# Layer two's weight conversions ordered behind the rectified tiles on ScalarE

## The chip, the cores and the metric

The kernel runs on one core of a Trainium2 chip. The metric is the device time of one launch in microseconds (us), the median of the runs that are shown. Five engines work beside each other: TensorE (PE, with its weight loads as PEld), VectorE (DVE), ScalarE (ACT), GpSimd (POOL) and SyncE (SP), which starts most transfers. Each engine executes its own instructions strictly in the order in which they were put.

## The reference

Three steps, all in float32:

```python
# 1. retention attention, 2 batches x 8 heads x 768 tokens x 64, in 12 blocks of 64 tokens
intra = (qb @ kb.T * Dmask) @ vb
inter = (qb * lam_pow) @ kv_state
out[block] = intra + inter
kv_state = lam_block * kv_state + (kb * rev_pow).T @ vb
# 2. x: (2, 768, 512), mixed by two Fourier transforms, then layer one
u = x + real(fft(fft(x, axis=1), axis=2))
un = (u - mean(u)) / sqrt(var(u) + 1e-6)
x = u + maximum(un @ w_ch1, 0) @ w_ch2          # 512 -> 2048 -> 512
# 3. layer two, with a gain g_ln and weights of its own
xn = (x - mean(x)) / sqrt(var(x) + 1e-6) * g_ln
return x + maximum(xn @ w_ch1, 0) @ w_ch2
```

## The kernel before

**Tiling.** The 1536 tokens are four blocks of 384. Each of the two layers runs over its four blocks, and each block over the 16 groups `f` of 128 hidden units. One step of that is a `unit(n)`, n = 0 to 127: layer n // 64, block n // 16 % 4, group n % 16. The last block of layer one is n = 48 to 63; names of it carry `0_3`, those of the first block of layer two `1_0`. A float32 operand is held as two float16 tiles, a high and a low part, and a product is three matmul passes over them.

**The way up.** `mlp_up_fast` (L826) takes two groups at once with seven block products in place of eight. I call two such groups a pair, and number the eight pairs of a block from 0 (pair k is f = 2k and 2k + 1). A product is 6 matmuls of 192 columns (L845) into two PSUM tiles: "left" holds the first 192 tokens (`ps_1...`, as `ps_11_0_12` for layer 1, block 0, f = 12), "right" the others (`ps_2...`). In the second half of a pair, ahead of `rest`, come product three and the product "12" into left, then VectorE forms `t` from left (L865) and adds it into right (L866). `rest` then puts the last left product (`th,w`) and the last right product (`unT,sw`), VectorE adds to left (L871) and to right (L872), ScalarE rectifies left and right into the high part of `h` (L877), and VectorE computes the low part (L878). So L865 reads what the last left product overwrites, and L866 what the last right product adds to.

**The way down.** `mlp_down` puts, three units later, the matmuls of 512 columns that read `h` (L892), 9 for a group.

**Sums.** The seven products need sums of weights (`w1_sums`: L790 on VectorE, L791 to L793 and L797 on GpSimd, L796 on ScalarE) and of normalized tokens (`un_sums`: L805, L810 to L813 on VectorE, L820 on ScalarE, L821 on GpSimd). A block's tokens are normalized before it starts: L706 and L714 on ScalarE, L715 on GpSimd, then transposes by SP into `unT`.

**Conversions.** Weights come from memory 512 columns at a time and are turned into high and low float16 parts by `conv_steps`, whose steps go from engine to engine: ScalarE L301 and L302 (into a PSUM tile), VectorE L304, ScalarE L326 (the gain, for layer two's first matrix) and L327 (high part), GpSimd L329 (low part). Layer two has 16 conversions of its first matrix (`w1_unit`, every second one followed by `w1_sums`) and 16 of its second. Six of the latter (`AWAY`) are made early in the kernel, stored to memory and loaded back; ten are converted in the stretch that this case is about.

**The order.** A list scheduler places every instruction on its engine in the order of a modelled time, by priority and by dependences. Background work is put at a unit number by `put` and recorded in the middle of that unit, after the pair's first products and before `mlp_down` and `rest`. `gate["relu"]` is the last rectification (L877) recorded so far; `tc.issue_after(x)` bars everything recorded under it from being placed ahead of x on ScalarE. Before, the conversions ran under `later`, which leaves them their priority and asks for no order; only the stagings of the six early tiles (`staged_late`) stood behind the rectification.

Of the kernel before, what the change touches and what calls it, by code (L numbers as in the profile page):

```python
# [51 lines left out]
EARLY0, GATEN, B1, SPC, DS, DC, DFO, DD, D1S, D2S, AO, YA, NR, NE, LN1, L1, L2, F01, F02, TL, R1, R2, SE, PR1, LAG, UB, FB, NW, MQ, SPL = 11, 8, 6, 2.0, 2.0, 5, 1.0, 0.5, 0.5, 1.0, "aba", "aa", 2, 0, 3, 2.5, 2.5, 16, 4, 3, 1.5, 2, "dddd_dppp", 0, 3, 3, 13, 11, 1, 3  # L52
# [3 lines left out]
AWAY = {0: 37, 2: 39, 4: 41, 6: 43, 8: 45, 10: 47}  # L56
# [67 lines left out]
def tile_retention_fourier_mlp(ctx: ExitStack, tc: tile.TileContext, a: dict, out: bass.AP):  # L124
# [28 lines left out]
    def hl(name):  # L153
        return fp.tile([P, 2, 512], F16, tag="f", name=name)
# [116 lines left out]
    def run(steps):  # L271
        for t in steps:
            pass
        return t

    def w_conv(kind, m, i):
        return run(conv_steps(kind, m, i, "at"))

    def w_stage(i):
        t = hl(f"wst2_{i}")  # L280
        run(conv_steps(2, 1, i, "at", t))
        away[i] = dram.tile([P, 2, 512], F16, name=f"wd{i}")
        sp.dma_start(away[i], t)

    def w_back(i):
        w2t[1, i] = wpool.tile([P, 2, 512], F16, tag=f"w2_{i}", name=f"w2_1_{i}")
        sp.dma_start(w2t[1, i], away[i])
# [393 lines left out]
    unT, unt, gate = {}, {}, {}  # L681
# [90 lines left out]
    def w1_sums(m, g, kk, r=None):  # L772
        w = w1t[m, g]
        i = (2 * g + kk - 2) % 8
        if 3 <= i < 7:
            t = const.tile([P, 2, 2, 2, 256], F16, tag=f"big{i - 3}", name=f"sw{m}_{g}_{kk}")
            t = [t[:, 0], t[:, 1]]
        elif i < 3:
            t = [ldp.tile([P, 2, 2, 256], F16, tag="ld", name=f"sw{m}_{g}_{kk}_{x}") for x in range(2)]
        else:  # L780
            t = [const.tile([P, 2, 2, 256], F16, tag=f"state{x}", name=f"sw{m}_{g}_{kk}_{x}") for x in range(2)]
        if r is None:
            r = [f32t(f"wr{m}_{g}_{k}") for k in (kk, kk + 2)]
            for x, k in enumerate((kk, kk + 2)):
                dve.tensor_tensor(r[x], w[:, 0, k], w[:, 1, k], op=ALU.add)  # L785
        eng = [pool if z == "p" else dve for z in SE.split("_")[m]]
        (a11, a21), (a12, a22) = ([z.rearrange("p (q a f) -> p q a f", a=2, f=P)[:, :, x] for x in range(2)] for z in r)
        s12, s34 = (f32t(f"ws{x}_{m}_{g}_{kk}") for x in (12, 34))
        s1, s2, s3, s4 = (z[:, x * 256:x * 256 + 256].rearrange("p (q f) -> p q f", f=P) for z in (s12, s34) for x in range(2))
        eng[0].tensor_tensor(s1, a21, a22, op=ALU.add)  # L790
        eng[1].tensor_tensor(s2, s1, a11, op=ALU.subtract)  # L791
        eng[2].tensor_tensor(s3, a11, a21, op=ALU.subtract)
        eng[3].tensor_tensor(s4, a12, s2, op=ALU.subtract)  # L793
        for x, z in enumerate((s12, s34)):
            hi, lo = (t[x][:, y].rearrange("p s f -> p (s f)") for y in range(2))
            act.copy(hi, z)  # L796
            pool.tensor_tensor(lo, z, hi, op=ALU.subtract)  # L797
        sw[m, g, kk] = t
# [254 lines left out]
    def put(n, task):  # L1053
        bg.setdefault(max(int(n), 0), []).append((n, len(bg), task))

    def later(task, offset):
        def run():
            with tc.high_priority(offset=-offset):
                task()
        return run  # L1060
# [21 lines left out]
    n = t + DC + DFO  # L1082
# [25 lines left out]
    n0 = (NB - 1) * NF  # L1108
    first = {}

    def w1_unit(p):
        g, kk, half = p // 4, p % 4 // 2, p % 2
        t = w_conv(1, 1, 4 * g + kk + 2 * half)
        if not half:
            first[g, kk] = t
        else:
            w1_sums(1, g, kk, (first.pop((g, kk)), t))

    for i in range(NF):
        put(n0 + 4 + R1 * i, later(lambda i=i: w1_unit(i), PR1))  # L1120
        put(n0 + 3.5 + R2 * i, later(lambda i=i: w_back(i) if i in AWAY else w_conv(2, 1, i), PR1))
    def staged_late(i):
        with tc.issue_after(gate["relu"].ins):
            w_stage(i)

    for i, n in AWAY.items():
        put(n, lambda i=i: staged_late(i))

    def step(n):
        m = n // (NB * NF)  # L1130
# [59 lines left out]
```

## Time and profile before

| | us |
|---|---|
| median of 3 runs | 589.38 |
| lowest and highest run | 588.20, 590.11 |
| profiled execution | 589.12 |
| its span | 587.3 |
| granted TensorE clock, mean share of full | 0.996 |
| PE busy | 568.8 (97%) |
| DVE busy | 390.1 (66%) |
| ACT busy | 279.9 (48%) |
| POOL busy | 280.7 (48%) |

All times of the profile run from the start of the span. The launch takes 1.8 us more than the span. The conversions of layer two lie between 293 and 400 us, in which layer one's last block ends (at some 340 us) and layer two's first block runs (to about 398 us). Busy shares over the whole span say that PE is the engine that is nearly always at work; what the others delay can be seen only as gaps on PE.

### The profile page before, as it was taken

The page shows a single profiled execution, that of the slowest core. Times are in us where ns is not written, and L with a number is a line of the kernel's source. Part 1 is how long each engine was busy: PE and PEld are TensorE (multiplying, and loading weights), DVE is VectorE, ACT ScalarE, POOL GpSimd, SP SyncE. Part 2 cuts the span into 40 slices and gives each one's busy share as a digit, 9 for nine tenths or more (in the row PEclk, how much of TensorE's full clock was granted, in tenths as well). Part 3 has the DMA queues.
Part 4 walks back from the last instruction along what each step waited for, and adds up shares of the span by engine and source line. Part 5 has one row for each costly group of instructions (what it writes and reads, how often), then busy time and mean ns, then how long its engine had stood idle before and what let it go on. Part 6 is the DMA issues. An engine that isn't in the chain of part 4 may idle for free.

```text
span 587.3 us, 11862 instructions
## 1 busy us (share of the span) xinstructions
PE 568.8 (97%) x4655; PEld 378.3 (64%) x4655; DVE 390.1 (66%) x868; ACT 279.9 (48%) x561; POOL 280.7 (48%) x294
## 2 busy tenths in 40 slices
PE   7889999999999999999999999999999999999997
PEld 5745645566554555676676676776767677767775
DVE  6998898766976449678767768666536453544333
ACT  3667779733332334455497787953223132312110
POOL 8935799985452564454476876952112100210000
PEclk8999999999999999999999999999999999999999
DMA  8998079960000010253265442700110025002001
GB/s 285 368 397 335 2 252 262 340 203 3 1 1 0 19 37 18 73 127 108 83 206 179 133 156 84 168 19 2 64 28 19 1 88 57 20 1 88 22 2 54
DMA packets 47014, 63.23 MB, mean 108 GB/s; under 512 B 26224, under 2 KB 29166, under 8 KB 46958
## 3 DMA queue, kind: packets, MB, share of 16 engines
q1 hardware_dynamic: 46142, 62.27, 34.2%
q8 instruction: 36, 0.59, 0.4%
q10 hardware_dynamic: 816, 0.21, 0.2%
q14 instruction: 20, 0.16, 0.1%
HBM read 52.23 MB, written 6.29 MB: 100 GB/s over the span
## 4 chain that ended last, share of the span: by engine, by line
PE 65%; DVE 12%; ACT 6%; POOL 6%; DMA 5%; issue 5%; SPq 1%; DVEq 0%; POOLq 0%; ACTq 0%
PE ps_y L892 30%; PE ps L845 22%; PE ps_h L752 6%; DMA k<-in_k 3%; POOL w L329 2%; PE ps_d L551 1%; ACT w L327 1%; POOL sw L797 1%; DVE wr L785 1%; PE ps_y_at L892 1%; PE ps_y_dn L892 1%; DMA cdsd<-in_cd 1%; DMA ws<-in_w 1%; ACT top L310 1%; DVE u L918 1%
## 5 line engine op out<-in xcount | busy, mean ns | idle before, releaser
L892 PE MATMUL ps_y<-w,h 128*128 128x512 f16 x1104 | 271.6, 379 | 2.4 <-ACT h L877 1.6
L892 PEld LDWEIGHTS <-h 128*128 128x128 f16 x1200 | 113.8, 98 | 100.6 <-ACT h L877 3.7
L845 PEld LDWEIGHTS <-sw 128*128 128x128 f16 x1104 | 94.5, 98 | 15.8 <-issue 3.0
L845 PE MATMUL ps<-th,sw 128*128 128x192 f16 x828 | 91.1, 246 | 1.1 <-DVE wf L304 0.7
L845 PEld LDWEIGHTS <-w 128*128 128x128 f16 x828 | 72.0, 98 | 17.1 <-issue 0.2
L877 ACT ACTIVATE h<-ps 128x384 f16<-128x384 f32 x92 | 43.6, 488 | 80.6 <-DVE ps L871 76.1
L329 POOL TENSOR_TENSOR w<-wf,w 128x512 f16<-128x512 f32 x58 | 66.8, 1160 | 22.6 <-ACT w L327 22.3
L752 PE MATMUL ps_h<-unT,w 128*128 128x384 f16 x396 | 72.5, 326 | 1.0 <-ACT w L327 0.8
L845 PE MATMUL ps<-unT,w 128*128 128x192 f16 x552 | 62.9, 246 | 0.0
L878 DVE SCALAR_TENSOR_TENSOR h<-ps,h 128x384 f16<-128x384 f32 x92 | 49.2, 554 | 13.9 <-ACT h L877 12.2
L752 PEld LDWEIGHTS <-w 128*128 128x128 f16 x396 | 37.6, 98 | 29.9 <-ACT w L327 1.7
L865 DVE TENSOR_TENSOR t<-ps,s 128x192 f32<-128x192 f32 x46 | 16.3, 354 | 54.0 <-PE ps L845 54.0
L797 POOL TENSOR_TENSOR sw<-ws,sw 128x512 f16<-128x512 f32 x32 | 37.0, 1173 | 21.2 <-ACT sw L796 21.2
L715 POOL TENSOR_TENSOR uns<-un,uns 128x512 f16<-128x512 f32 x21 | 25.2, 1198 | 39.3 <-ACT uns L714 39.3
L694 POOL TENSOR_TENSOR rs<-rs,neghalf 128x1 f32<-128x1 f32 x24 | 14.4, 603 | 61.9 <-DVE rs L692 59.6
L327 ACT CAST w<-wf 128x512 f16<-128x512 f32 x58 | 35.2, 611 | 11.9 <-DVE wf L314 8.8
L821 POOL TENSOR_TENSOR th<-ts,th 128x384 f16<-128x384 f32 x24 | 22.1, 939 | 38.8 <-ACT th L820 38.8
L857 ACT COPY s<-ps 128x192 f32<-128x192 f32 x46 | 14.4, 313 | 53.8 <-PE ps L845 53.7
L871 DVE TENSOR_TENSOR ps<-ps,s 128x192 f32<-128x192 f32 x46 | 16.6, 360 | 29.3 <-PE ps L845 29.1
L379 POOL TENSOR_TENSOR m<-m,m 128x512 f16<-128x512 f32 x24 | 31.5, 1327 | 4.7 <-ACT m L377 4.6
L304 DVE SCALAR_TENSOR_TENSOR wf<-ws,ps_w 128x512 int32<-128x512 int32 x34 | 23.2, 684 | 14.8 <-ACT ps_w L302 8.8
L767 DVE SCALAR_TENSOR_TENSOR h<-ps_h,h 128x384 f16<-128x384 f32 x36 | 19.7, 550 | 18.7 <-ACT h L766 18.6
(176 smaller groups left out, 851.1 us busy)
## 6 DMA issues: line engine op xcount, KB each, us to landing
ws<-in_w SPq DMA_DIRECT2D x25, 511.8 KB, 5.4
ws<-in_w2b SPq DMA_DIRECT2D x16, 511.8 KB, 4.3
ws<-in_w1b SPq DMA_DIRECT2D x16, 511.8 KB, 3.9
kt<-in_kt SPq DMA_DIRECT2D x12, 256.0 KB
qt<-in_qt SPq DMA_DIRECT2D x12, 256.0 KB, 5.3
v<-in_v SPq DMA_DIRECT2D x12, 256.0 KB
k<-in_k SPq DMA_DIRECT2D x12, 256.0 KB, 5.2
pre<-in_w SPq DMA_DIRECT2D x4, 511.8 KB
```

Of the source, the lines that this page charges most:

```text
L304: dve.scalar_tensor_tensor(ti, raw[:, :, 0], 13, part.bitcast(I32), op0=ALU.logical_shift_right, op1=ALU.bitwise_or)
L327: act.copy(hi, t)
L329: gate["lo"] = pool.tensor_tensor(lo, t, hi, op=ALU.subtract)
L379: pool.tensor_tensor(t[:, 1], m32, t[:, 0], op=ALU.subtract)
L715: pool.tensor_tensor(s_[:, 1], un, s_[:, 0], op=ALU.subtract)
L752: pe.matmul(ps, w[:, i, k, fo:fo + P], x[:, j, k, :], start=n == 0, stop=n == 11)
L797: pool.tensor_tensor(lo, z, hi, op=ALU.subtract)
L821: pool.tensor_tensor(t[:, 1], z, t[:, 0], op=ALU.subtract)
L845: pe.matmul(ps, lhs, rhs, start=start and n == 0, stop=n == 5, skip_group_check=True)
L877: gate["relu"] = act.activation(hi, z, AF.Relu)
L878: dve.scalar_tensor_tensor(lo, z, 0.0, hi, op0=ALU.max, op1=ALU.subtract)
L892: pe.matmul(ps, h[:, x, j * P:(j + 1) * P], w[:, y, c], start=f == 0 and n == 0, stop=f == NF - 1 and n == 2)
```

## The change

All 16 conversions of the first matrix and the 10 of the second now run under `issue_after(gate["relu"].ins)`, as the stagings did. The loads of the six stored tiles (`w_back`) lose `later` too. No operation is added or taken away; what each engine executes is put in another order.

```diff
+    def behind_relu(task, i):
+        with tc.issue_after(gate["relu"].ins):
+            task(i)
+
     for i in range(NF):
-        put(n0 + 4 + R1 * i, later(lambda i=i: w1_unit(i), PR1))
-        put(n0 + 3.5 + R2 * i, later(lambda i=i: w_back(i) if i in AWAY else w_conv(2, 1, i), PR1))
-    def staged_late(i):
-        with tc.issue_after(gate["relu"].ins):
-            w_stage(i)
-
+        put(n0 + 4 + R1 * i, lambda i=i: behind_relu(w1_unit, i))
+        put(n0 + 3.5 + R2 * i, lambda i=i: w_back(i) if i in AWAY else behind_relu(lambda i: w_conv(2, 1, i), i))
     for i, n in AWAY.items():
-        put(n, lambda i=i: staged_late(i))
+        put(n, lambda i=i: behind_relu(w_stage, i))
```

Here `n0` is 48, `R1` is 1.5 and `R2` is 2, so that a conversion of the first matrix is put every 1.5 units from unit 52 on, and one of the second at every second unit from 51 on.

On ScalarE, in layer two's first block, these rows stand between the right rectification of pair 1 (h1_0_1 from ps_21_0_2) and the left one of pair 2 (h1_0_2 from ps_11_0_4). Names end in a buffer number; `half`, `ps_w` and `wf` are tiles of a conversion (`1_1_12` is the twelfth of layer two's first matrix, `2_1_9` one of its second), `sw` is a sum of weights, `un` and `uns` are normalized tokens. Before:

```order
L877 ACTIVATE h1_0_1_4901<-ps_21_0_2_4814 128x2x192
L706 ACTIVATE un1_1_0_4982<-u0_119,rs1_1_0_4933 128x512
L796 CAST sw1_2_1_4947<-ws34_1_2_1_4949 128x512
L302 CAST ps_w1_1_12_5057<-half1_1_12_5056 128x512
L714 CAST uns1_1_0_4986<-un1_1_0_4982 128x512
L857 COPY s1_0_6_5030<-ps_11_0_6_5031 128x192
L301 ACTIVATE half1_1_13_5206<-ws1_1_13_5203 128x512
L326 ACTIVATE wf1_1_12_5055<-wf1_1_12_5055,gcol_187 128x512
L302 CAST ps_w1_1_14_5102<-half1_1_14_5101 128x512
L877 ACTIVATE h1_0_2_5025<-ps_11_0_4_4907 128x2x192
```

After, behind the same right rectification of pair 1:

```order
L301 ACTIVATE half1_1_11_4939<-ws1_1_11_4936 128x512
L301 ACTIVATE half2_1_9_4994<-ws2_1_9_4991 128x512
L302 CAST ps_w1_1_11_4940<-half1_1_11_4939 128x512
L302 CAST ps_w2_1_9_4995<-half2_1_9_4994 128x512
L326 ACTIVATE wf1_1_11_4938<-wf1_1_11_4938,gcol_187 128x512
L327 CAST w2_1_9_4999<-wf2_1_9_4993 128x512
L327 CAST w1_1_2_4722<-wf1_1_11_4938 128x512
L706 ACTIVATE un1_1_0_4982<-u0_119,rs1_1_0_4933 128x512
L796 CAST sw1_2_1_4947<-ws12_1_2_1_4948 128x512
L714 CAST uns1_1_0_4986<-un1_1_0_4982 128x512
L857 COPY s1_0_6_5030<-ps_11_0_6_5031 128x192
L877 ACTIVATE h1_0_2_5025<-ps_11_0_4_4907 128x2x192
```

Eleven instructions stand between the two rectifications in place of eight, seven of them a whole stage of two conversions; and conversion 11 stands where 12 to 14 stood before.

On PE, pair 6 of the same block: the rows from the end of the product "12" (`unT,w` into `ps_11_0_12`) on. `ps_11_0_14` is the next pair's left tile, `ps_y` the way down. Before:

```order
L845 MATMUL ps_11_0_12_5377<-unT1_0_3886,w1_1_3_5061 128x192
L892 LDWEIGHTS h1_0_5_5371
L892 MATMUL ps_y1_0_1_4876<-w2_1_10_5096,h1_0_5_5371 128x512
L892 LDWEIGHTS h1_0_5_5371
L892 MATMUL ps_y1_0_2_4877<-w2_1_10_5096,h1_0_5_5371 128x512
L845 LDWEIGHTS w1_1_3_5061
L845 MATMUL ps_11_0_14_5479<-unT1_0_3886,w1_1_3_5061 128x192
L845 LDWEIGHTS w1_1_3_5061
L845 MATMUL ps_11_0_14_5479<-unT1_0_3886,w1_1_3_5061 128x192
```

After:

```order
L845 MATMUL ps_11_0_12_5377<-unT1_0_3886,w1_1_3_5061 128x192
L845 LDWEIGHTS w1_1_3_5061
L845 MATMUL ps_11_0_12_5377<-th1_1_0_0_4324,w1_1_3_5061 128x192
L845 LDWEIGHTS w1_1_3_5061
L845 MATMUL ps_11_0_12_5377<-th1_1_0_1_4438,w1_1_3_5061 128x192
```

Before, 11 matmuls of 512 columns and 8 of 192 lay between the product "12" and the last left product `th,w`; now the one follows the other with none between. Behind the pair's last right product, 13 matmuls of the next products came before the first matmul that reads `h1_0_6`; now none. In pair 7 the rows after the change stand in the same way, where 22 matmuls lay between the two left products before.

On VectorE at the same place (`tr` and `ts` are the sums of the next block's tokens, `un_sums`). Before:

```order
L865 TENSOR_TENSOR t1_0_13_5420<-ps_11_0_12_5377,s1_0_12_5376 128x192
L805 TENSOR_TENSOR tr1_1_0_5423<-unT1_1_4985 128x384
L805 TENSOR_TENSOR tr1_1_2_5425<-unT1_1_4985 128x384
L866 TENSOR_TENSOR ps_21_0_12_5378<-ps_21_0_12_5378,t1_0_13_5420 128x192
L810 TENSOR_TENSOR ts12_1_1_0_5427<-tr1_1_0_5423 128x192
L812 TENSOR_TENSOR ts34_1_1_0_5428<-tr1_1_2_5425,tr1_1_0_5423 128x192
L811 TENSOR_TENSOR ts12_1_1_0_5427<-tr1_1_2_5425,ts12_1_1_0_5427 128x192
L813 TENSOR_TENSOR ts34_1_1_0_5428<-tr1_1_2_5425,ts12_1_1_0_5427 128x192
L871 TENSOR_TENSOR ps_11_0_12_5377<-ps_11_0_12_5377,s1_0_12_5376 128x192
```

After:

```order
L865 TENSOR_TENSOR t1_0_13_5420<-ps_11_0_12_5377,s1_0_12_5376 128x192
L805 TENSOR_TENSOR tr1_1_0_5423<-unT1_1_4985 128x384
L805 TENSOR_TENSOR tr1_1_2_5425<-unT1_1_4985 128x384
L866 TENSOR_TENSOR ps_21_0_12_5378<-ps_21_0_12_5378,t1_0_13_5420 128x192
L810 TENSOR_TENSOR ts12_1_1_0_5427<-tr1_1_0_5423 128x192
L871 TENSOR_TENSOR ps_11_0_12_5377<-ps_11_0_12_5377,s1_0_12_5376 128x192
L812 TENSOR_TENSOR ts34_1_1_0_5428<-tr1_1_2_5425,tr1_1_0_5423 128x192
```

The two L805 stand between L865 and L866 in both; L871 has moved ahead of three of the sums.

## Rows read from the trace of the kernel before

**Rows 1.** Page, part 1: busy us, share of the span, instructions.
```profile
PE 568.8 (97%) x4655; PEld 378.3 (64%) x4655; DVE 390.1 (66%) x868; ACT 279.9 (48%) x561; POOL 280.7 (48%) x294
```

**Rows 2.** Stretches: us, PE, PEld, DVE, ACT, POOL busy, granted clock, DMA share, GB/s.
```profile
293.00:325.00 32.00, 31.04 (x251) 21.50 (x249) 23.46 (x51) 25.68 (x51) 21.83 (x23) 1.00 0.55 177
325.00:350.00 25.00, 24.29 (x196) 16.91 (x194) 17.00 (x39) 21.08 (x42) 19.32 (x21) 1.00 0.52 157
350.00:375.00 25.00, 24.58 (x205) 17.50 (x203) 19.97 (x48) 20.11 (x40) 18.22 (x21) 1.00 0.54 135
375.00:400.00 25.00, 24.87 (x203) 17.52 (x201) 17.81 (x44) 15.54 (x32) 16.43 (x17) 1.00 0.14 38
```

**Rows 3.** Waits of PE, 225 to 400 us: total, times, longest.
```profile
PE ps_y L892 <- ACT h L877: 1.6, 3, 0.8
PE ps L845 <- DVE wf L304: 0.7, 1, 0.7
```

**Rows 4.** Timeline at three gaps of PE: start, us, engine, operation [idle before <-releaser].
```profile
320.44 0.72 ACT L326 ACTIVATE wf<-wf,gcol 128x512 f32<-128x512 f32 x1 [1.57 <-DVE wf L304]
...
322.93 1.25 PE L892 MATMUL ps_y<-w,h 128*128 128x512 f16 x5 [0.79 <-ACT h L877]
...
329.68 1.15 PE L845 MATMUL ps<-th,sw 128*128 128x192 f16 x12 [0.71 <-DVE wf L304]
...
353.27 0.87 ACT L877 ACTIVATE h<-ps 128x384 f16<-128x384 f32 x2 [1.39 <-DVE ps L871]
```

**Rows 5.** Timeline of a pair without conversions, layer two's second block.
```profile
440.28 0.66 PE L845 MATMUL ps<-th,w 128*128 128x192 f16 x6
...
440.77 0.66 PE L845 MATMUL ps<-unT,sw 128*128 128x192 f16 x6
440.98 0.37 DVE L871 TENSOR_TENSOR ps<-ps,s 128x192 f32<-128x192 f32 x1 [1.67 <-PE ps L845]
...
441.38 0.98 ACT L877 ACTIVATE h<-ps 128x384 f16<-128x384 f32 x2 [2.47 <-DVE ps L871]
```

**Rows 6.** ScalarE's groups, 293 to 400 us: count, busy us, mean ns, idle before.
```profile
L301 ACT ACTIVATE half<-ws 128x512 f16<-128x512 bf16 x24 | 16.1, 673 | 0.9 <-DMA ws<-in_w2b 0.7
L302 ACT CAST ps_w<-half 128x512 f32<-128x512 bf16 x26 | 15.1, 583 | 8.4 <-DVE h L878 7.0 <-DVE wf L304 1.3
L327 ACT CAST w<-wf 128x512 f16<-128x512 f32 x25 | 15.1, 612 | 0.9 <-DVE wf L304 0.8
...
L326 ACT ACTIVATE wf<-wf,gcol 128x512 f32<-128x512 f32 x16 | 11.5, 718 | 1.9 <-DVE wf L304 1.6
L796 ACT CAST sw<-ws 128x512 f16<-128x512 f32 x16 | 9.8, 613 | 2.7 <-POOL ws L791 1.5 <-POOL ws L793 1.2
L857 ACT COPY s<-ps 128x192 f32<-128x192 f32 x14 | 4.3, 306 | 0.0
...
L714 ACT CAST uns<-un 128x512 f16<-128x512 f32 x4 | 2.5, 614 | 0.0
L706 ACT ACTIVATE un<-u,rs 128x512 f32<-128x512 f32 x3 | 2.4, 809 | 0.0
```

**Rows 7.** PE, then VectorE, in pair 6 of layer two's first block.
```profile
391.95 0.66 PE L845 MATMUL ps<-unT,w 128*128 128x192 f16 x6
...
392.65 0.36 DVE L865 TENSOR_TENSOR t<-ps,s 128x192 f32<-128x192 f32 x1 [1.59 <-PE ps L845]
392.92 1.02 DVE L805 TENSOR_TENSOR tr<-unT 128x384 f32<-128x384 f16 x2
393.86 0.36 DVE L866 TENSOR_TENSOR ps<-ps,t 128x192 f32<-128x192 f32 x1
394.12 0.35 DVE L810 TENSOR_TENSOR ts<-tr 128x192 f32<-128x192 f32 x1
```

**Rows 8.** The same sums for the block before, beside GpSimd.
```profile
314.94 2.27 POOL L797 TENSOR_TENSOR sw<-ws,sw 128x512 f16<-128x512 f32 x2
...
316.27 1.82 DVE L805 TENSOR_TENSOR tr<-unT 128x384 f32<-128x384 f16 x2
```

## The prediction, made before the changed kernel was run

> **What bounds the kernel now.** I read the page's busy shares first, then PE's stretches, then PE's waits, then the timeline at its gaps. PE is busy for 568.8 us, 97% of the span, and no other engine for more than 66% [rows 1]; so the time can change only through gaps on PE. Between 293 and 400 us, where the conversions run, PE works at the full clock (2.4 GHz) for 31.04 + 24.29 + 24.58 + 24.87 = 104.78 of 107 us [rows 2]. The gaps are thus 2.2 us, and this is all that better placing could win. PE's waits name nearly all of it: 1.6 us in three waits for the rectified tile, 0.7 us in one for a conversion's L304 [rows 3]. The timeline tells why. At 322.93 PE waited 0.79 us for h, since ScalarE had itself stood 1.57 us before the gain L326, waiting for VectorE's L304, with the rectification queued behind it; at 329.68 it waited 0.71 us behind the same L304 [rows 4]. Both lie in layer one's last block, together 1.5 us.
>
> **The price of a short distance.** Matmuls of 192 columns start 0.082 us apart (440.28 to 440.77 for six), so one of 512 columns takes 0.218. In a pair that no conversion disturbs, the last left matmul starts at 440.28 + 5 x 0.082 = 440.69, L871 at 440.98, and the rectifications take 0.98 for two, so the left one ends at 441.38 + 0.49 = 441.87 [rows 5]. The way is 1.18 us: if PE has less than that to do between a pair's last left product and the first matmul that reads its h, it stands. Before the change nearly all pairs had 1.5 to 4 us there by the order.
>
> **The change part by part.** Every operation stays, so nothing is removed but waits, and PE's work is the same. What moves:
>
> *Layer one's last block, gain.* Conversions no longer interleave freely with its rectifications; each starts behind one. The waits of 0.79 and 0.71 us came from a conversion step placed ahead of the rectification or of L858/L872 in VectorE's queue [rows 4]. I take 1.1 of the 1.5 us as won, since in the new order pairs 6 and 7 of this block have only 18 matmuls (1.5 us) in the distance and eight to nine conversion steps ahead of their rectifications. Bounds: 1.5 won, or nothing.
>
> *Pair 2 of layer two's first block, loss.* The wait that the change adds stands here. Eleven ScalarE instructions lie between the right rectification of pair 1 and the left one of pair 2. Their durations are 2 x 0.673 + 2 x 0.583 + 0.718 + 2 x 0.612 + 0.809 + 0.613 + 0.614 + 0.306 = 6.80 us [rows 6]. Two successive ones overlap by 0.1 (0.87 for two of 0.48 to 0.49) [rows 4, 5], so 5.7, and 0.49 for the rectification: 6.2. I add 0.3, as L326 waits for L304, which starts only when the first L302 is done and lasts longer than the second one that covers it; over the stretch L326 waited 1.9 us in 16 [rows 6]. Against it PE has, from pair 1's last right matmul to the first that reads h of pair 2, 31 x 0.082 + 18 x 0.218 = 6.45 us by the new order (54 and 18 in the old). The right rectification of pair 1 ends at the earliest 1.18 behind that matmul, so PE stands 1.18 + 6.2 + 0.3 - 6.45 = 1.2 us. Bounds: the distance in pair 2 is seven starts (0.57 us), so 0.6 is the least; 2.0 if L326 waits as long as at 320.44 once more.
>
> *Pair 5, loss.* The distance is ten matmuls, 11 x 0.082 = 0.90, so at least 0.3. Ahead of its rectification stand L706, a sum's L796 and L714 (0.61 each), whose inputs come from POOL; I put half of one, 0.3, on the path. 0.6, bounds 0.3 and 1.2.
>
> *Pairs 6 and 7, loss.* The last left product follows the product "12" without a matmul between. The product's last start is 391.95 + 5 x 0.082 = 392.36, L865 starts 0.29 behind and ends at 393.01 [rows 7]; it reads what the next product overwrites, which else would start at 392.44. PE stands about 0.65. VectorE then does both L805 and L866, which ends at 394.22, 1.86 behind that last start [rows 7]; PE has meanwhile had 0.49 of left product from 0.73 on, to 1.22, so the right product waits 0.65 more. L810 takes the next 0.27, L871 starts at about 2.03 and ends at 2.40, the left rectification at 2.9; the right product is through at 2.4, so 0.5 to 0.55. Sum 1.85 for a pair, 3.7 for two. Before, the same VectorE chain lay beside 11 + 8 matmuls (3 us) and cost 0.3 at most in the whole block's end (a 0.13 us gap in 25 us of busy PE, [rows 2], and up to 0.17 of it hidden in the modelled end of a matmul): net 3.4. Bounds: 0.6 a pair, 1.2 in all, if the other engines are ahead of PE there, so that the sums are done before L865 is due and only the short way to h is left; and the cost of rows 8 twice, next.
>
> *Beside POOL.* VectorE's two L805 took 1.02 us at 392.92 [rows 7], but 1.82 at 316.27 while POOL worked on L797 until 317.21 [rows 8]. With sums and low parts moved later, such a meeting can fall on pairs 6 and 7: 0.8 each, 1.6 in all. The Trainium skill (SBUF — State Buffer, section "Who interferes with whom") says that a VectorE instruction with two SBUF inputs and a GpSimd one that reads SBUF share a port and that the later one is blocked until the other is done. The rows agree in direction: L805 reads two SBUF operands and grew by 0.8 while L797 ran. By this rule the sum would be 1.6 higher if both pairs met POOL; I take none, since POOL has few conversions left by then (16.43 us of 25 busy, 375 to 400, and it falls further behind).
>
> *SP and the transfers.* SP's order changes by 34 rows: loads of raw weights come when their staging tiles are free, and transposes of `unT` behind L714 and L715. ScalarE's L301 waited 0.7 us in all for loads, 24 of them [rows 6], and DMA is busy 0.14 to 0.55 [rows 2]; I cost the loads at nothing. If `unT` comes so late that L805 waits, pairs 6 and 7 pay directly, as L866 stands behind; this belongs to the worse rival.
>
> Sum: 1.2 + 0.6 + 3.4 - 1.1 = +4.1 us. On the profiled execution's 589.12 that is 593.2; that execution lies 0.26 below the median of 589.38, within the runs' spread of 588.2 to 590.1.
>
> **The rivals.**
> *Faster.* The rectifications, freed of conversions ahead of them, never come late, the gaps of [rows 3] go and the short distances are filled because PE falls behind nothing: 589.1 - 2.2 = 586.9. For it: two of the four waits do come from conversion steps. Against: the order leaves no matmul between product and use in pairs 2, 6 and 7, and no engine can close 1.18 us of round trip. Chance 0.09.
> *No difference.* Only the least losses are paid, 0.6 + 0.3 + 1.2, against 1.5 to 2.2 won: 589.1 + 2.1 - 1.8 = 589.4. It needs VectorE and ScalarE to be ahead of PE by a pair's work when pair 6 comes. For it: PE, once delayed, lets them catch up, so the later losses may shrink. It also holds the case that the change does little, as conversions mostly stood behind a rectification anyhow; against that, the new order differs from the old in 303 lines on ScalarE. Chance 0.21.
> *Worse.* The next block's `unT` or the sums come so late that VectorE stands in pairs 6 and 7 with L866 and L871 queued behind, or POOL blocks L805 there; nothing is won before. 593.2 + 1.6 + 1.1 = 595.9. It decides as soon as the transposes end later than L865 is due; before, both L805 began right behind L865, with no wait [rows 7]. Chance 0.15.
> *Forecast*, 591.1 to 595: chance 0.55.
>
> **How the numbers follow.** A measurement of this kernel can tell about 0.3%, 1.8 us. Slower by more than that holds the forecast and the worse rival, 0.70; within, 0.21; faster, 0.09. The range: the low end is the case with no difference, 589.0, the high one the worse rival, 596.0; below it lies the faster case, about 0.1, above it less.
>
> **What would show it.** Right: PE's waits between 275 and 400 us grow from 2.3 to about 6, with new ones at L845 for VectorE's L865 and L866 and at L892 for L877 in pairs 2, 6 and 7 of layer two's first block; the stretch 350 to 400 us loses 3 to 5 us of busy PE, and the 1.57 us stand of L326 is gone or lies behind a rectification. Wrong: PE's busy time there stays at 24.6 to 24.9 of 25 in spite of the short distances, which would mean that other engines run ahead far enough; or the loss sits in the clock, which I expect to stay at 1.00.

## The result: 1.2% slower

| | us |
|---|---|
| before, median of 5 runs | 589.29 |
| changed, median of 5 runs (595.10 to 597.23) | 595.65 |
| ratio, with its 95% interval | 1.0120 (1.0105 to 1.0134) |

The medians are 6.4 us apart, the ratio gives 7.1 (6.2 to 7.9). The forecast was +4.1 us, 593.2, with 589 to 596: the side was right and the size too small. The median lies just inside the range; by the ratio, which compares runs taken together, the time is 596.4 and lies just above it. The changed kernel's profiled execution took 597.23, the slowest of its runs. About 1.4 us of its distance to before lies ahead of 225 us, where the change moves nothing; the comparison of stretches below starts at 293.

The changed kernel's stretches, against [rows 2] (the last one, 400 to 425, had 24.92 us of busy PE before):

```profile
293.00:325.00 32.00, 30.84 (x250) 21.25 (x248) 23.61 (x47) 22.11 (x44) 20.20 (x21) 1.00 0.47 148
325.00:350.00 25.00, 23.80 (x191) 16.33 (x190) 17.24 (x39) 19.98 (x39) 16.81 (x18) 1.00 0.41 127
350.00:375.00 25.00, 23.57 (x186) 15.98 (x185) 19.68 (x45) 19.91 (x40) 17.34 (x19) 1.00 0.40 137
375.00:400.00 25.00, 24.25 (x194) 16.62 (x192) 13.07 (x33) 18.46 (x36) 19.95 (x21) 1.00 0.39 107
400.00:425.00 25.00, 21.97 (x182) 15.50 (x182) 16.46 (x44) 9.55 (x21) 5.98 (x6) 1.00 0.09 33
```

PE lost work in every stretch, most behind 400 us; the granted clock stayed at 1.00. The prediction looked for 3 to 5 us lost between 350 and 400; it was 1.6 there and 2.95 behind 400, where pairs 6 and 7 now end. PE's waits from 225 to 420 us, against [rows 3]:

```profile
PE ps_y L892 <- ACT h L877: 2.4, 7, 0.4
PE ps_y L892 <- DMA ws<-in_w1b: 1.1, 1, 1.1
PE ps L845 <- DVE s L858: 1.1, 1, 1.1
PE ps L845 <- DVE ps L866: 1.1, 2, 0.6
PE ps_y L892 <- DVE h L878: 1.0, 1, 1.0
PE ps L845 <- DVE t L865: 1.0, 2, 0.5
```

2.3 us in four waits have become 7.7 in fourteen. The two for L865 and the two for L866 are the forecast ones in pairs 6 and 7; the one put down to a load is really one for h (below).

**Two blocks apart.** The waits leave out what the modelled end of a matmul hides. So I also summed, over all matmuls from 275 to 425 us, the time from one start to the next less the matmul's columns at 2.4 GHz. I call this the stands, and cut it at 345 us, about where layer two's first block takes over:

| stands, us | layer one's last block | layer two's first block |
|---|---|---|
| before | 4.3 | 2.9 |
| changed | 4.8 | 9.0 |
| forecast change | -1.1 | +5.2 |
| measured change | +0.4 | +6.1 |

The sum, +6.5, agrees with the 6.4 us between the medians. This table is the thread through the experiments.

**Pair 2** went as worked out. ScalarE and PE, between the right rectification of pair 1 and the left one of pair 2:

```profile
363.08 0.49 ACT L877 ACTIVATE h<-ps 128x384 f16<-128x384 f32 x1 [0.99 <-DVE ps L872]
363.47 1.22 ACT L301 ACTIVATE half<-ws 128x512 f16<-128x512 bf16 x2
...
365.98 0.72 ACT L326 ACTIVATE wf<-wf,gcol 128x512 f32<-128x512 f32 x1 [0.30 <-DVE wf L304]
...
369.60 0.86 ACT L877 ACTIVATE h<-ps 128x384 f16<-128x384 f32 x2
...
370.13 0.11 PEld L892 LDWEIGHTS <-h 128*128 128x128 f16 x2 [1.34 <-ACT h L877]
370.13 0.60 PE L892 MATMUL ps_y<-w,h 128*128 128x512 f16 x2 [1.12 <-DMA ws<-in_w1b]
```

From 363.47 ScalarE works through the eleven instructions with one gap of 0.30, the forecast wait for L304, and is done with the left rectification at about 370.08. The matmul's row names a load, but its weight load beside it names the rectification: of several semaphores the row shows one. The stand is 1.28 us, forecast 1.2.

**Pair 6** of the same block, PE, VectorE and ScalarE:

```profile
399.07 0.66 PE L845 MATMUL ps<-unT,w 128*128 128x192 f16 x6
399.77 0.36 DVE L865 TENSOR_TENSOR t<-ps,s 128x192 f32<-128x192 f32 x1 [1.24 <-PE ps L845]
400.04 1.02 DVE L805 TENSOR_TENSOR tr<-unT 128x384 f32<-128x384 f16 x2
400.18 0.66 PE L845 MATMUL ps<-th,w 128*128 128x192 f16 x6 [0.45 <-DVE t L865]
400.98 0.36 DVE L866 TENSOR_TENSOR ps<-ps,t 128x192 f32<-128x192 f32 x1
...
401.39 0.66 PE L845 MATMUL ps<-unT,sw 128*128 128x192 f16 x6 [0.55 <-DVE ps L866]
401.51 0.36 DVE L871 TENSOR_TENSOR ps<-ps,s 128x192 f32<-128x192 f32 x1
...
401.90 0.49 ACT L877 ACTIVATE h<-ps 128x384 f16<-128x384 f32 x1 [3.77 <-DVE ps L871]
...
402.45 0.60 PE L892 MATMUL ps_y<-w,h 128*128 128x512 f16 x2 [0.40 <-ACT h L877]
...
403.38 0.82 PE L892 MATMUL ps_y<-w,h 128*128 128x512 f16 x3 [0.33 <-ACT h L877]
```

The chain runs step for step as forecast: L865, two L805, L866, the right product, L871, L877, h. PE stands three times for the left half, 0.61 + 0.72 + 0.57 us with the hidden parts, where the forecast had 0.65, 0.65 and 0.55. The fourth stand, 0.50 at 403.38 for the right half's h, was not in it.

### The profile page after: what moved, and what is told of

It reads as the page before. It is cut to its first block, busy times and chain, and to the rows that moved or that the text cites. A ratio compares the mean times of both kernels' runs of the same rounds, so it can differ in the third digit from the quotient of the medians.

```text
span 595.4 us, 11853 instructions
## 1 busy us (share of the span) xinstructions
PE 570.5 (96%) x4655; PEld 378.6 (64%) x4655; DVE 389.7 (65%) x868; ACT 280.6 (47%) x561; POOL 281.5 (47%) x294
## 4 chain that ended last, share of the span: by engine, by line
PE 62%; POOL 12%; DVE 12%; ACT 7%; issue 5%; DMA 2%; SPq 0%; DVEq 0%; POOLq 0%
PE ps_y L892 29%; PE ps L845 21%; PE ps_h L752 5%; POOL w L329 4%; POOL m L379 3%; POOL kd L341 1%; PE ps_d L551 1%; ACT h L877 1%; ACT w L327 1%; PE ps_h L742 1%; DVE wr L785 1%; PE ps_y_at L892 1%; PE ps_y_dn L892 1%; DVE wf L304 1%; ACT wf L326 1%
## 5 line engine op out<-in xcount | busy, mean ns | idle before, releaser
L845 PE MATMUL ps<-th,sw 128*128 128x192 f16 x828 | 92.4, 246 | 1.2 <-DVE s L858 1.1
L877 ACT ACTIVATE h<-ps 128x384 f16<-128x384 f32 x92 | 44.1, 490 | 93.6 <-DVE ps L871 88.0
L329 POOL TENSOR_TENSOR w<-wf,w 128x512 f16<-128x512 f32 x58 | 67.2, 1171 | 22.1 <-ACT w L327 21.9
L865 DVE TENSOR_TENSOR t<-ps,s 128x192 f32<-128x192 f32 x46 | 16.2, 353 | 53.7 <-PE ps L845 53.6
L797 POOL TENSOR_TENSOR sw<-ws,sw 128x512 f16<-128x512 f32 x32 | 37.3, 1179 | 21.4 <-ACT sw L796 21.4
L821 POOL TENSOR_TENSOR th<-ts,th 128x384 f16<-128x384 f32 x24 | 22.2, 943 | 42.8 <-ACT th L820 41.3
L871 DVE TENSOR_TENSOR ps<-ps,s 128x192 f32<-128x192 f32 x46 | 16.6, 361 | 33.4 <-PE ps L845 33.3
L845 PE MATMUL ps<-th,w 128*128 128x192 f16 x276 | 30.8, 246 | 1.1 <-DVE t L865 1.0
```

What stands on the lines that cost most here:

```text
L329: gate["lo"] = pool.tensor_tensor(lo, t, hi, op=ALU.subtract)
L821: pool.tensor_tensor(t[:, 1], z, t[:, 0], op=ALU.subtract)
L845: pe.matmul(ps, lhs, rhs, start=start and n == 0, stop=n == 5, skip_group_check=True)
L877: gate["relu"] = act.activation(hi, z, AF.Relu)
```

## Why layer one's last block won nothing

Pair 4 of that block, VectorE and GpSimd in the changed kernel:

```profile
316.01 0.35 DVE L865 TENSOR_TENSOR t<-ps,s 128x192 f32<-128x192 f32 x1
316.17 0.72 POOL L791 TENSOR_TENSOR ws<-ws,wf 128x256 f32<-128x256 f32 x1 [3.28 <-DVE ws L790]
316.28 2.46 DVE L805 TENSOR_TENSOR tr<-unT 128x384 f32<-128x384 f16 x2
316.86 2.90 POOL L329 TENSOR_TENSOR w<-wf,w 128x512 f16<-128x512 f32 x2
318.66 0.35 DVE L866 TENSOR_TENSOR ps<-ps,t 128x192 f32<-128x192 f32 x1
318.93 1.04 DVE L810 TENSOR_TENSOR ts<-tr 128x192 f32<-128x192 f32 x1
319.72 0.84 POOL L793 TENSOR_TENSOR ws<-wf,ws 128x256 f32<-128x256 f32 x1
319.89 0.88 DVE L812 TENSOR_TENSOR ts<-tr,tr 128x192 f32<-128x192 f32 x1
320.51 1.27 POOL L797 TENSOR_TENSOR sw<-ws,sw 128x512 f16<-128x512 f32 x1
320.69 1.30 DVE L811 TENSOR_TENSOR ts<-tr,ts 128x192 f32<-128x192 f32 x1
...
322.32 0.66 PE L845 MATMUL ps<-th,sw 128*128 128x192 f16 x6 [1.11 <-DVE s L858]
```

The GpSimd work of two conversions and of their weight sums now comes as one block, 316.2 to 321.8, and the five token sums of these rows lie in it: 2.46 + 1.04 + 0.88 + 1.30 = 5.7 us in place of the 2.1 that two L805 (1.02) and three sums of 0.35 take alone. GpSimd's own rows grow too (L329 from 1.16 to 1.45 each). L858 stands behind them, and PE waits for it. L866 and L865, which read PSUM, stay at 0.35. The ends show that the two engines take turns, one instruction each: L810, L812 and L811 each end 0.21 us after the GpSimd row that was already running ended (319.97 against 319.76, 320.77 against 320.56, 321.99 against 321.78), and L797 ends 1.01 after L812. The Trainium skill (SBUF — State Buffer, "Who interferes with whom") says that a VectorE instruction with two SBUF inputs contends with a GpSimd instruction that reads SBUF. The rows agree.

The same meeting was in the kernel before, and I had read past it. Four of its rows, not shown above:

```profile
316.96 0.58 ACT L302 CAST ps_w<-half 128x512 f32<-128x512 bf16 x1
...
318.17 1.16 POOL L329 TENSOR_TENSOR w<-wf,w 128x512 f16<-128x512 f32 x1 [0.95 <-ACT w L327]
...
318.29 1.25 DVE L810 TENSOR_TENSOR ts<-tr 128x192 f32<-128x192 f32 x1
...
319.73 0.68 DVE L304 SCALAR_TENSOR_TENSOR wf<-ws,ps_w 128x512 int32<-128x512 int32 x1
```

L810 took 0.9 us more than alone, the L805 of [rows 8] 0.8. L304 had its input at 317.54, when L302 ended, but was queued behind both and started at 319.73; L326 stood 1.57 us for it [rows 4]. So the wait at 322.93, which the forecast put down to a conversion step ahead of the rectification, began with VectorE's sums. The wait at 329.68 is not behind the same L304, as the forecast has it, but behind one of the next pair, which has the second set of token sums ahead of it (L805 of 0.84 and 1.08 us, L813 of 0.77).

## The experiments

Sixteen kernels, all timed; "stands" are for the two blocks as above (before 4.3 and 2.9, changed 4.8 and 9.0). Ratios, with their intervals, are to the kernel before as it was timed again beside each group of runs (588.8 to 588.9 us).

**1 and 2. One matrix at a time.**

```diff
-        put(n0 + 3.5 + R2 * i, lambda i=i: w_back(i) if i in AWAY else behind_relu(lambda i: w_conv(2, 1, i), i))
+        put(n0 + 3.5 + R2 * i, later(lambda i=i: w_back(i) if i in AWAY else w_conv(2, 1, i), PR1))
```

> Only the 16 conversions of layer two's first matrix are ordered behind the rectification, the 10 of the second run as in the kernel before. Theory A (the first matrix's conversions and the sums that follow them are late, and that leaves PE without cover in pairs 2, 5, 6 and 7 of layer two's first block): the order keeps all four short distances, so the loss stays, 595 to 596.5 us. Rival B (the number of conversions behind one rectification decides, ScalarE is simply too full there): ten of 26 are free again, a third or more of the 6.4 us comes back, 592 to 593.5.

599.64 us, 1.0174 (1.0151 to 1.0198), stands 4.8 and 13.3. The loss did not stay, it grew, beyond both expectations: besides pairs 2, 6 and 7, PE stood 1.4 us more for L858 and 0.7 for a late weight sum. At half the clock PE lost another 1.7 us behind the 1.4 (last section). B is out; A fits the place of the loss but not its size, and no run shows why the first matrix alone costs more than both.

```diff
-        put(n0 + 4 + R1 * i, lambda i=i: behind_relu(w1_unit, i))
+        put(n0 + 4 + R1 * i, later(lambda i=i: w1_unit(i), PR1))
```

> The mirror image: only the 10 conversions of the second matrix are ordered behind the rectification. Theory A: no pair of the two blocks has less than 1.5 us of matmuls between its last left product and the first matmul that reads its h, so nothing of the loss, 588 to 590.5 us. Rival B: ten of 26 ordered, 591 to 592.

590.12 us, 1.0016 (1.0001 to 1.0031), stands 6.0 and 2.9: A. Layer two's first block is free of the loss, so the first matrix's order makes all of it there. Layer one's last block has 1.7 us more, as much as a stretch at half the clock cost there (last section).

**5. Neither order nor `later`.**

```diff
-        put(n0 + 4 + R1 * i, lambda i=i: behind_relu(w1_unit, i))
-        put(n0 + 3.5 + R2 * i, lambda i=i: w_back(i) if i in AWAY else behind_relu(lambda i: w_conv(2, 1, i), i))
+        put(n0 + 4 + R1 * i, lambda i=i: w1_unit(i))
+        put(n0 + 3.5 + R2 * i, lambda i=i: w_back(i) if i in AWAY else w_conv(2, 1, i))
```

> No conversion is ordered behind the rectification, and none is recorded under later either: the other half of the change by itself. Theory A (lateness by the order decides): 588 to 590.5 us, as the kernel before. The order of PE has two places without cover ahead of the last left product (pairs 2 and 4 of layer two's first block, 0.49 and 0.08 us between the product 12 and it), priced as pairs 6 and 7 of the changed kernel without the two L805 at 0.65 each, so up to 591. Rival: dropping later is what moved the conversions, 594 or more.

590.14 us, 1.0030 (1.0019 to 1.0041), stands 4.2 and 4.3, as A expected. Of the 1.2% of the whole change, 0.3 comes with dropping `later` alone (as it does without the order).

**3. The last sums early.**

```diff
-        put(n0 + 4 + R1 * i, lambda i=i: behind_relu(w1_unit, i))
+        put(n0 + 4 + R1 * i - (3 if i > 11 else 0), lambda i=i: behind_relu(w1_unit, i))
```

> The changed kernel, with the last four conversions of the first matrix (number 12 to 15) put three units earlier, still behind a rectification. The order on PE is the same up to pair 2 of layer two's first block; pairs 5, 6 and 7 have 2.5 to 4 us between product and use again, and 3 us of cover before the last left product. Theory A (lateness of the last sums): the stands of pairs 5 to 7, 0.77 + 2.4 + 1.97 us in the changed kernel's trace, go, about 4.8 net of what the kernel before had there: 590.5 to 591.5. Rival C (the order behind the rectification itself costs, and the loss moves to other pairs): 594 to 596.

594.69 us, 1.0082 (1.0060 to 1.0104), stands 4.6 and 8.2. Pairs 5 to 7 lost their stands, as A said, but PE then stood 1.42 us for L304, 0.97 for L865 and 0.58 for h by pairs 2 and 3, where the four conversions had gone, and lost 3.0 us more at half the clock, which set in behind the first of these (last section). The result is C's, but the gaps themselves, 3.0 us, are fewer than the 4.8 that went.

**8. The next block's token sums early.**

```diff
-                put(at - TL + 2 * kk if (m, blk) != (1, 0) else at - 7 + 2 * kk, lambda m=m, blk=blk, kk=kk: un_sums(m, blk, kk))
+                put(at - TL - (1 if m == 1 and blk == 1 else 0) + 2 * kk if (m, blk) != (1, 0) else at - 7 + 2 * kk, lambda m=m, blk=blk, kk=kk: un_sums(m, blk, kk))
```

> The changed kernel, with the token sums of layer two's second block put one unit earlier. By the order, pair 7 of the first block has 3.1 us of cover ahead of its last left product again and 2.5 us before h; pair 6 has none ahead of the product, but 1.5 us before h. Price of the round trips as the changed kernel's trace has them: pair 7's 1.97 us go, and pair 6's two waits for h of 0.57 and 0.50: 592.6 us. If the sums are themselves too early (unT not there), VectorE stands in pair 6 and the loss stays: 595 or more.

595.73 us, 1.0113 (1.0096 to 1.0130), stands 4.8 and 9.3. Pair 7 was free, but the first L805 waited 3.31 us for the transposes into `unT`, with pair 6's L858 and L865 behind it, and 1.7 us more went at half the clock. The normalized tokens of the next block are late as well as the weights' sums.

**4 and 9. GpSimd's reads taken out in pair 4,** of the changed kernel and of the one before. The four writes depend on nothing then, and GpSimd makes them earlier, so that in pair 4 only its other reads (L791 and L793 in the changed kernel) are left. PE's and VectorE's order is unchanged in the changed kernel (one L796 stands three places further up on ScalarE), and differs in a few rows in the other.

```diff
-        gate["lo"] = pool.tensor_tensor(lo, t, hi, op=ALU.subtract)
+        gate["lo"] = pool.memset(lo, 0.0) if (m, i) == (1, 3) else pool.tensor_tensor(lo, t, hi, op=ALU.subtract)
...
-            pool.tensor_tensor(lo, z, hi, op=ALU.subtract)
+            pool.memset(lo, 0.0) if (m, g, kk) == (1, 0, 1) else pool.tensor_tensor(lo, z, hi, op=ALU.subtract)
```

> The changed kernel with the same order on every engine; four GpSimd instructions in pair 4 of layer one's last block (the low parts of conversion 3 of both matrices, L329 twice, and of one pair of weight sums, L797 twice) set their tile to zero in place of reading two tiles and subtracting. These low parts are left out of the computation. Theory D (VectorE's sums L805 to L812 there took 0.9 to 1.5 us in place of 0.35 to 0.55 because GpSimd reads at the same time): they come down by 2 to 3 us together, the stand of 1.28 us of PE before ps_10_3_10 goes, 594 to 594.6 us. Rival E (they are long for another reason, such as the transposes or PE's reads): the same durations and 595.6.

593.31 us, 1.0071 (1.0052 to 1.0089), stands 2.2 and 9.0. VectorE in the same place:

```profile
318.77 0.34 DVE L810 TENSOR_TENSOR ts<-tr 128x192 f32<-128x192 f32 x1
319.04 0.35 DVE L812 TENSOR_TENSOR ts<-tr,tr 128x192 f32<-128x192 f32 x1
319.30 0.35 DVE L811 TENSOR_TENSOR ts<-tr,ts 128x192 f32<-128x192 f32 x1
319.57 0.35 DVE L858 TENSOR_TENSOR s<-ps,s 128x192 f32<-128x192 f32 x1
```

D is right on the mechanism: the three sums are back at 0.35, L858 comes 2.35 us earlier, and 2.5 us of stands are gone, more than D's range of times had. The two L805 still took 1.04 and 1.08 us, beside L791 and L793. But does it explain the difference?

> The kernel before, with the same four GpSimd instructions setting their tile to zero as in the run of the changed kernel (low parts of conversion 3 of both matrices and of one pair of weight sums of layer two; left out of the computation). Theory D: before, VectorE's sums beside them lost less (L805 once 1.36 in place of 0.55, L810 1.25 in place of 0.35), and the waits at 320.46 and 322.93, 1.2 us, hang on them: 587.8 to 588.8, a gain of 0.2 to 1.2 against 2.3 in the changed kernel. If the gain is as large as there (2 us or more), GpSimd's reads cost both kernels alike and do not explain the difference.

586.54 us, 0.9958 (0.9943 to 0.9974), stands 2.0 and 2.8. The gain is as large as in the changed kernel, so by the mark set beforehand the meeting does not explain why the changed kernel is slower. It explains why the block won nothing: both kernels paid for it there, 2.3 us of stands before and 2.5 after. With the reads gone, the waits of [rows 4] at 320.44 to 329.68 are gone, though the conversions stand among the rectifications as before:

```profile
314.82 1.01 DVE L805 TENSOR_TENSOR tr<-unT 128x384 f32<-128x384 f16 x2
...
316.02 0.35 DVE L810 TENSOR_TENSOR ts<-tr 128x192 f32<-128x192 f32 x1
...
317.27 0.72 ACT L326 ACTIVATE wf<-wf,gcol 128x512 f32<-128x512 f32 x1
...
319.26 0.86 ACT L877 ACTIVATE h<-ps 128x384 f16<-128x384 f32 x2
```

**6 and 13. All two units early.**

```diff
-        put(n0 + 4 + R1 * i, lambda i=i: behind_relu(w1_unit, i))
-        put(n0 + 3.5 + R2 * i, lambda i=i: w_back(i) if i in AWAY else behind_relu(lambda i: w_conv(2, 1, i), i))
+        put(n0 + 2 + R1 * i, lambda i=i: behind_relu(w1_unit, i))
+        put(n0 + 1.5 + R2 * i, lambda i=i: w_back(i) if i in AWAY else behind_relu(lambda i: w_conv(2, 1, i), i))
```

> The changed kernel with all conversions of both matrices put two units earlier, still ordered behind a rectification. All pairs of the two blocks have 1.5 us or more between product and h again, and all but one 1.3 us or more ahead of the last left product. Theory A (lateness): 589 to 591 us. Theory C (a batch of conversion steps behind a rectification holds up the next one wherever it stands, as the run with the last sums early suggests): six to ten rectifications have 1.5 us alone and ScalarE's batch ahead, 592 to 596 us.

595.76 us, 1.0116 (1.0097 to 1.0134), stands 9.6 and 3.9. By the time alone C is right. By the stands the loss changed its block: layer two's is nearly cured, layer one's doubled (1.7 us of it at half the clock), and there the rows are of the other kind:

```profile
328.58 2.59 POOL L797 TENSOR_TENSOR sw<-ws,sw 128x512 f16<-128x512 f32 x2
328.78 2.81 DVE L805 TENSOR_TENSOR tr<-unT 128x384 f32<-128x384 f16 x2
331.14 2.69 POOL L329 TENSOR_TENSOR w<-wf,w 128x512 f16<-128x512 f32 x2
...
332.75 1.30 DVE L812 TENSOR_TENSOR ts<-tr,tr 128x192 f32<-128x192 f32 x1
...
334.63 0.57 PE L845 MATMUL ps<-th,sw 128*128 128x192 f16 x5 [2.06 <-DVE s L858]
```

Runs 13 to 15 decide between the two, with a larger set of GpSimd's parts set to zero (`m == 1 and 3 <= i <= 6`, and the sums `(1, 0, 1)` and `(1, 1, 0)`) in the early, the changed and the kernel before. A few places in PE's order change with it: 25, 8 and 6 of the 4655 matmuls in the traces.

> All conversions two units earlier, ordered behind the rectification (595.8 us with its work whole), and GpSimd's low parts of conversions 3 to 6 of both matrices and of two pairs of weight sums set to zero in place of being computed; this part is left out. Theory F (two separate costs: lateness, which leaves PE without cover in pairs 2, 5, 6 and 7 of layer two's first block, and which two units earlier cures; and VectorE's token sums beside GpSimd in layer one's last block, which took over there, 6.4 us of stands): the stands in layer one's last block fall to 1 to 2 us and nothing comes back in layer two's, 589.5 to 591.5. Theory C (the batch behind a rectification costs wherever it stands): no more gain than in the other two kernels, 592.5 to 593.5.

> The changed kernel with the same, larger set of GpSimd's parts left out, as the measure for the two runs beside it. Layer one's last block then keeps at most 0.6 us of its stands (0.6 with the smaller set), layer two's its 6.9: 592 to 593.3.

> The kernel before with the same, larger set left out. With the smaller set nothing but 0.3 us of stands was left in layer one's last block, so the same again: 586 to 587. The difference to the changed kernel with this set then is the order's price without the sums' meeting with GpSimd: 5.5 to 7 us by theory F, less than 4 if the meeting explains a part of it.

| larger set left out | us | ratio | stands, two blocks |
|---|---|---|---|
| early | 589.13 | 1.0009 (1.0000 to 1.0019) | 3.3, 3.9 |
| changed | 591.84 | 1.0062 (1.0045 to 1.0078) | 1.5, 9.0 |
| before | 586.42 | 0.9958 (0.9946 to 0.9971) | 1.7, 2.8 |

F holds against C, though not every number of it: the early kernel gains 6.6 us, the changed one 3.8, the one before 2.4. F had 1 to 2 us of stands left in the early kernel's first block, and it has 3.3. Two L805 in the early one:

```profile
325.38 1.02 DVE L805 TENSOR_TENSOR tr<-unT 128x384 f32<-128x384 f16 x2
```

Without these parts the changed order costs 591.84 - 586.42 = 5.4 us, all in layer two's first block (9.0 against 2.8), while layer one's shows 1.5 against 1.7. That is 1.0 us less than the 6.4 of the whole kernels (0.7 by the stands), which the intervals hardly tell from nothing: the meeting explains little of the difference, if any. Two units earlier the order costs 589.13 - 586.42 = 2.7. So half of its price is lateness. By the stands, the earlier order takes 5.1 of the 6.2 us in layer two's first block away and adds 1.9 in layer one's last (3.33 against 1.47); why it costs there, no run shows.

**Tries at something better (7, 10, 11, 12, 16).** All move the token sums of layer two's first block by a unit, from 7 units ahead of the block to 8 or 6 (16 also orders GpSimd's part of later conversions behind L821):

```diff
-                put(at - TL + 2 * kk if (m, blk) != (1, 0) else at - 7 + 2 * kk, lambda m=m, blk=blk, kk=kk: un_sums(m, blk, kk))
+                put(at - TL + 2 * kk if (m, blk) != (1, 0) else at - 8 + 2 * kk, lambda m=m, blk=blk, kk=kk: un_sums(m, blk, kk))
```

> The changed kernel, with the token sums of layer two's first block (un_sums) put one unit earlier, so that VectorE's L805 to L813 stand by pair 3 of layer one's last block in place of pair 4; all is computed, and the order on PE is unchanged in pairs 2 to 7 of layer two's first block. Theory D: they fall where GpSimd has fewer reads to do, take less than 1 us more than alone, and of the 2.3 us that the run with GpSimd's writes only gave, 1 to 2.3 us come back: 593.3 to 594.7. Otherwise they meet GpSimd again and 595 to 596.5.

> Only the second matrix's conversions ordered behind the rectification, and the token sums of layer two's first block one unit later: a try at a kernel better than both. No pair has less than 1.5 us between product and h. In the run with the second matrix alone PE stood 1.9 us behind L813 and L811 beside GpSimd. Theory D: if the sums now miss GpSimd's reads, that stand and the low clock behind it go, 586.5 to 588; if they meet them again, 589 to 591.

> The kernel before with only the token sums of layer two's first block one unit later, the other half of that try. 587 to 588.5 if the waits at 320.46 to 329.68 (2.1 us with that of L304) go with the sums' meeting with GpSimd; 589 to 591 if they meet elsewhere.

> As the try with the second matrix alone, but the token sums of layer two's first block one unit earlier than in the kernel before. Theory D as there: 586.5 to 588 if the sums miss GpSimd's reads, 589 to 591 if not.

> A try at a kernel better than both, all computed: only the second matrix's conversions behind the rectification, the token sums of layer two's first block one unit earlier, and GpSimd's part of every conversion that follows them in the program ordered behind GpSimd's own part of the token sums (L821), so that it cannot read while VectorE makes these sums. If this parts the two, the 1.3 us of stands of the run without that order go: 586.5 to 587.5. If GpSimd's parts then come late for the weight sums, 588.5 to 591.

| run | kernel, units ahead | us | ratio | stands |
|---|---|---|---|---|
| 7 | changed, 8 | 597.14 | 1.0136 (1.0113 to 1.0159) | 5.1, 8.5 |
| 10 | second matrix alone, 6 | 589.39 | 1.0008 (0.9995 to 1.0021) | 3.8, 3.5 |
| 11 | before, 6 | 592.66 | 1.0069 (1.0044 to 1.0093) | 8.0, 3.2 |
| 12 | second matrix alone, 8 | 588.24 | 0.9995 (0.9982 to 1.0007) | 3.1, 2.8 |
| 16 | as 12, GpSimd ordered | 591.79 | 1.0047 (1.0030 to 1.0064) | 4.7, 3.2 |

None beats the kernel before; run 12 equals it. In 7 and 11 the sums met GpSimd again, and both came out slower than expected for that case; in 16 the parts held back ran together, beside the second set of sums, whose L805 took 1.54 and 1.08 us. Whether the 2.4 us that the meeting costs can be won with everything computed stays open.

## Why the prediction was right in its side and wrong in its size

- *What bounds the kernel:* right. PE's work and its clock between 293 and 425 us did not change, only its gaps.
- *Layer one's last block, -1.1 us:* this step failed. It put the waits at 322.93 and 329.68 down to "a conversion step placed ahead of the rectification or of L858/L872 in VectorE's queue", so that the new order would take them away. Measured +0.4. Run 9 shows that they came from the token sums beside GpSimd, and run 4 that the new order keeps that meeting, at 2.5 us of stands. The text had [rows 8] and weighed them for pairs 6 and 7, where the changed kernel's trace has no such meeting: right row, wrong place. This is 1.5 us of the miss.
- *Pair 2, +1.2:* 1.28, by the chain that was worked out.
- *Pair 5, +0.6:* 0.57 for h and 0.20 for the weight sum.
- *Pairs 6 and 7, +3.4 net:* the chain was right, its size 0.9 too small. The two pairs stood 2.6 and 2.0 us, less the 0.3 of before: 4.3. Left out were the right half's h in pair 6 (0.5) and a wait for L858 ahead (0.2).
- *Beside POOL in pairs 6 and 7, nothing taken:* right, L805 took 1.02 us for two.
- *Transfers at nothing:* right. The one wait that a row puts down to a load is one for h.
- *The rival "worse"* had the total (595.9) by luck. It was right that nothing is won before, but its other 1.6 us were to come from `unT` or GpSimd in pairs 6 and 7, and neither came; longer chains in those pairs filled their place.

## What to carry to other kernels

Ordering background work behind the instruction that the busiest engine waits for protects that one instruction and can make what lies downstream late and bunched (here the first matrix's conversions and sums; the second matrix's order alone cost layer two's block nothing). Look for the place where the late product is needed, and count the matmuls that the order leaves between a result and its first use. Where they are fewer than the round trip (here 1.18 us), the stand can be priced before the run from the order and a quiet pair. Before a wait is credited to the instruction named beside it, compare durations of one line with its own minimum: a queue that is late because its instructions are longer is not cured by another order.

## What the runs showed of the hardware

VectorE's token sums, which read two SBUF operands, and GpSimd's instructions that read SBUF took turns, not only in pair 4 of the changed kernel: in the 18 traces, from 230 us on, 143 token sums began while a GpSimd instruction ran and took longer than alone, and 142 of them ended 0.41 to 0.42 us (L805) or 0.21 to 0.22 us (L810 to L813) behind the end of that instruction. A 128x192 sum so went from 0.35 to as much as 1.3 us.

TensorE's granted clock fell behind some of the longer stands of the experiments, and never in the changed kernel's profile between 293 and 425 us. In run 2 PE stood 1.77 us for h at 331.25. The matmuls behind it, and the stretch in the columns of [rows 2]:

```profile
331.25 2.83 PE L892 MATMUL ps_y<-w,h 128*128 128x512 f16 x7 [1.77 <-ACT h L877]
```

```profile
331.00:335.00 4.00, 3.75 (x14) 1.98 (x15) 2.34 (x5) 3.86 (x8) 3.82 (x4) 0.58 0.03 10
```

The mean clock is 0.58: most of the 512-column matmuls there start 0.43 us apart in place of 0.21, which is the 1.2 GHz level. At 0.58 over 4 us it cost run 2 about 1.7 us, as much as the stand itself. In run 7 a stand of 1.95 us at 323.69 had full speed behind it:

```profile
324.00:328.00 4.00, 4.00 (x33) 2.76 (x32) 2.63 (x7) 3.70 (x8) 2.07 (x3) 1.00 0.06 6
```

and in run 16 one of 2.41 us had too. In runs 1, 3, 6, 8 and 11 the level fell as well, behind or during two or three stands close together that came to 1.9 to 3.2 us; it cost 1.5 to 1.7 us each time, and 3.0 in run 3. Yet the stand of run 7 also had two others close ahead of it, 0.66 and 0.56 us, which makes 3.2 in all. What tells the two kinds apart is not settled by these runs.
